# A cubic polynomial in place of tanh, with a general version behind a branch

## The chip, the cores and the metric

The kernel runs on one core of a Trainium2 chip. The core has TensorE for matmuls (PE in the rows; PEld is its weight load), VectorE (DVE), ScalarE (ACT), GpSimd (POOL) and SyncE (SP), whose queue issues most of the DMA transfers. The metric is the time of one execution on the device, in microseconds (us). The median of several runs is compared.

## The reference

Sigmoid attention with a shift by log S, and behind it a block of two matmuls with h - tanh(h) between them:

```python
scores = scale * np.matmul(q, k.transpose(0, 1, 3, 2)) - np.log(S)   # (8, 12, 448, 64) each
attn = 1.0 / (1.0 + np.exp(-scores))
attn_out = np.matmul(attn, v)
x = attn_out.transpose(0, 2, 1, 3).reshape(B * S, H * D)             # 3584 x 768
h = x @ w_in                                                         # 768 x 2048
g = h - np.tanh(h)
out = g @ w_out                                                      # 2048 x 768
```

q and k are drawn as normal values times about 0.42, v times 0.1. w_in and w_out are 64-bit floats, scaled by one over the root of their rows.

## The kernel before

The eight batches (448 tokens each) go through one after another. In batch b the first product (`moe1`, in `product`) makes h in eight groups of two 128-row blocks, in a PSUM tile ph; after each group `mix` turns it into g. The second product (`moe2`) makes the six output blocks po, d = 0 to 5, each from 16 blocks f of g, three matmuls each. Values are split into a high and a low float16 half, so each product is three matmuls of 448 columns.

Between the matmuls of `moe2` of batch b stand the steps of the attention of batch b + 1 (the generator `stream`: scores, sigmoid a, its halves ahl, the product acc, norms sqn and pbn). They are placed by hand: BLOCKS lists the positions at which the next step is issued, and `second` merges these events into the loop over the matmuls. From batch 1 on the last two f of d = 0 come in the middle of d = 1. Batch 0 is different: `first` follows a string of letters, ORDER, in which the 64-bit weights are converted (raw, stb, wo, wi), the first product runs in float32 and the attention of batch 1 is threaded in.

TensorE, ScalarE, VectorE and GpSimd execute what is issued to them in that order. SyncE's queue is in order too; in batch 0 the scheduler of the framework sets it. Tiles come from pools: the tag "mm" is a ring of two PSUM buffers that the po tiles take in turn, "sc" a ring of two for scores and ph, and "t" in the pool temps a ring of eight SBUF buffers for the temporaries of `mix`, the a and ahl of the attention and raw weights. A tile that takes a buffer waits until what the buffer held has been read.

`mix` before computes two things for a group: th = h - tanh(h), and a polynomial of degree eleven, h^3 times two quadratic factors in u = h^2. Where u is over 0.65^2, a predicated copy takes th. `finish_g` splits the group before into halves g.

Of the kernel before, what the change touches and what calls it, by code (L numbers as in the profile page):

```python
# [24 lines left out]
CUT = 0.65  # L25
# [3 lines left out]
KAPPA = 0.00592396  # L29
B1, C1 = 0.62576354, 2.54375998**2  # L30
B2, C2 = -2.38756233, 1.58089437**2


class Builder:
# [225 lines left out]
    def w_in_scales(self):  # L260


        nc = self.nc
        n = self.DFF // 4
        cn = self.ps.tile([P, 512], F32, name="cn", tag="av", bufs=1)
        for j, sq in enumerate(self.row):
            nc.tensor.matmul(cn[32 * j : 32 * (j + 1), :n], self.onesb[:, :32], sq, start=True, stop=True)
        st = self.sm.tile([P, 1], F32, name="st", tag="st")
        nc.vector.tensor_reduce(st, cn[:, :n], axis=AX.X, op=ALU.max)
        yield 0  # L270
        pt = self.ps.tile([P, 512], F32, name="pt", tag="tr", bufs=1)
        nc.tensor.transpose(pt[:1, :P], st, self.ident)
        mx = self.sm.tile([1, 1], F32, name="mx2", tag="mx2")
        nc.vector.tensor_reduce(mx, pt[:1, :P], axis=AX.X, op=ALU.max)
        yield 0
        pb = self.ps.tile([P, 512], F32, name="pb", tag="tr", bufs=1)
        nc.tensor.matmul(pb[:, :1], self.onesf[:1, :], mx, start=True, stop=True)
        self.W2 = self.const.tile([P, 1], F32, name="W2")
        nc.vector.tensor_scalar(self.W2, pb[:, 0:1], 1.03, None, op0=ALU.mult)
        self.Swi, self.iSwi = self.scale_of(self.W2, "swi")  # L280

    def w_out_bound(self, e):

# [352 lines left out]
        do_av()  # L636
        yield 1150, True

    def attention32(self):

        nc = self.nc
        tags = (("kn", "qn"), ("K", "Q"))
        loaded, todo, accs = [], [], {}
        xs = self.xs = []
        order = iter([(j, c) for j in range(self.NP) for c in (range(QT) if j % 2 else range(QT + 1))])

        def load():
            j = len(loaded)
            loaded.append(self.load_qk(0, j, tags[j % 2]))

        def values():
            l = next(l for l in loaded if len(l) == 2)
            l.append(self.load_v(0, loaded.index(l), self.att, "vhl", 3))

        def table():
            one = self.sm.tile([P, 1], F32, name="one", tag="m")
            nc.scalar.activation(one, self.nls, AF.Sigmoid)

        def scores():
            j, c = next(order)  # L660
            both = (j, j + 1) if c == QT else (j,)
            K, Q = ([loaded[i][x][:, None] for i in both] for x in range(2))
            a = self.weigh(self.scores(K, Q, c), 1.0 / math.sqrt(D))
            todo.append((j, c, a))

        def open_acc(j):
            accs[j] = self.ps.tile([P, 512], F32, name="acc", tag="mm", bufs=2)

        def av():
            j, c, a = todo.pop(0)  # L670
            v = loaded[j][2][:, None]
            if c == QT:
                open_acc(j + 1)
                self.av([accs[j], accs[j + 1]], v, a, c, 0)
            else:
                if c == 0 and j % 2 == 0:
                    open_acc(j)
# [28 lines left out]
    def h_scales(self, ix):  # L706

        V = self.nc.vector
        t1 = lambda name: self.sm.tile([P, 1], F32, name=name)
        ih, ihk = t1("ih"), t1("ihk")  # L710
        V.tensor_tensor(ih, ix, self.iSwi, op=ALU.mult)
        V.tensor_scalar(ihk, ih, KAPPA, None, op0=ALU.mult)
        return ih, ihk

    def split_x(self, hl, x, Sx, act):
# [21 lines left out]
    def g_scales(self, m):  # L737

        t1 = lambda name: self.sm.tile([P, 1], F32, name=name)
        V = self.nc.vector  # L740
        hb = t1("hb")
        V.tensor_scalar(hb, m, self.W2, None, op0=ALU.mult)
        hc = t1("hc")
        V.tensor_scalar(hc, hb, 1e12, None, op0=ALU.min)
        h2 = t1("h2")
        V.tensor_tensor(h2, hc, hc, op=ALU.mult)
        h3 = t1("h3")
        V.scalar_tensor_tensor(h3, h2, 1.0 / 9.0, hc, op0=ALU.mult, op1=ALU.mult)
# [54 lines left out]
    def mix(self, ps, g, ih, ihk):  # L803

        nc = self.nc
        V = nc.vector
        temp = lambda name: self.tp.tile([P, 2, self.S], F32, name=name, tag="t")
        u = temp("u")
        nc.scalar.activation(u, ps, AF.Square, scale=ih)  # L809
        th = temp("th")  # L810
        nc.scalar.activation(th, ps, AF.Tanh, scale=ih)  # L811
        m = temp("m")
        V.scalar_tensor_tensor(m, ps, ihk, u, op0=ALU.mult, op1=ALU.mult)  # L813
        V.scalar_tensor_tensor(th, ps, ih, th, op0=ALU.mult, op1=ALU.subtract)  # L814
        yield 1
        self.finish_g()
        yield 1
        q1 = temp("q1")
        nc.scalar.activation(q1, u, AF.Square, bias=self.b1)  # L819
        V.scalar_tensor_tensor(m, q1, C1, m, op0=ALU.add, op1=ALU.mult)  # L820
        yield 1
        q2 = temp("q2")
        nc.scalar.activation(q2, u, AF.Square, bias=self.b2)  # L823
        V.scalar_tensor_tensor(m, q2, C2, m, op0=ALU.add, op1=ALU.mult)  # L824
        yield 1
        nc.scalar.activation(u, u, AF.Relu, bias=self.b3)  # L826
        V.copy_predicated(m, u.bitcast(U32), th)  # L827
        yield 1
        self.late.append((m, g))

    def finish_g(self):
        while self.late:
# [62 lines left out]
    def build(self):  # L895
        nc, tc = self.nc, self.tc

        def const(name, value, n=1):
            t = self.const.tile([P, n], F32, name=name)
            nc.vector.memset(t, value)  # L900
            return t

        self.nls = const("nls", -math.log(self.S))
        self.b1 = const("b1", B1)
        self.b2 = const("b2", B2)
        self.b3 = const("b3", -CUT * CUT)
        self.tiny = const("tiny", TINY)
        self.ih0 = const("ih0", 1.0)
        self.ihk0 = const("ihk0", KAPPA)
        self.iSwo = const("iswo", 1.0, 2)  # L910
        self.sums = [const(f"ss{i}", 0.0, 6) for i in range(2)]
        self.Swo = []
        self.sums_out, self.bound = [[], []], [None, None]
        self.xs32, self.x2b = False, []
        pieces = list(self.pieces())
        nA = 4 * self.NC
        E = mybir.EngineType
        with tc.manual_schedule(engines={E.PE, E.Activation, E.DVE, E.Pool}):
            nB = nA + self.NF + self.EARLY
            self.stage = tc.alloc_tile_pool(name="stage", bufs=2, reuse_waits="tile")  # L920
            self.blocks = self.stream()
            self.first(
                self.convert(pieces[:nA], "attention"),
                self.convert(pieces[nA:nB], "mixture"),
                self.convert(pieces[nB:], "product"),
            )
        with tc.manual_schedule(engines={E.PE, E.Activation, E.DVE, E.Pool, E.SP}):
            for b in range(1, self.B):
                self.batch(b)
        self.gp.release()  # L930
# [128 lines left out]
    def second(self, b, blocks, alone, events):  # L1059

        step = lambda: next(self.blocks)
        events += [(p, step) for p in blocks]
        scales = []

        def norms():
# [12 lines left out]
        assert not events  # L1078


def build_kernel(tc, q, k, v, moe_w_in, moe_w_out, out):
    with ExitStack() as ctx:
        Builder(ctx, tc, q, k, v, moe_w_in, moe_w_out, out).build()


# [27 lines left out]
```

## Time and profile before

| What | Value |
| --- | --- |
| median of 3 runs | 1164.04 us (1163.76 to 1164.43) |
| span of the traced execution, from its first to its last instruction | 1163.1 us |
| TensorE busy | 1150.5 us (99%) |
| VectorE busy | 903.6 us (78%) |
| ScalarE busy | 865.6 us (74%) |
| GpSimd busy | 78.4 us (7%) |
| TensorE's weight loads busy | 555.4 us (48%) |

The traced execution has no time of its own beside its span; the runs' median is 0.94 us above it. An engine's busy time is the union of its instructions; matmuls are pipelined, so a busy TensorE may still have small waits between matmuls.

### The profile page before, as it was taken

The page shows a single profiled execution, that of the slowest core. Times are in us where ns is not written, and L with a number is a line of the kernel's source. Part 1 is how long each engine was busy: PE and PEld are TensorE (multiplying, and loading weights), DVE is VectorE, ACT ScalarE, POOL GpSimd, SP SyncE. Part 2 cuts the span into 40 slices and gives each one's busy share as a digit, 9 for nine tenths or more (in the row PEclk, how much of TensorE's full clock was granted, in tenths as well). Part 3 has the DMA queues.
Part 4 walks back from the last instruction along what each step waited for, and adds up shares of the span by engine and source line. Part 5 has one row for each costly group of instructions (what it writes and reads, how often), then busy time and mean ns, then how long its engine had stood idle before and what let it go on. Part 6 is the DMA issues. An engine that isn't in the chain of part 4 may idle for free.

```text
span 1163.1 us, 17369 instructions
## 1 busy us (share of the span) xinstructions
PE 1150.5 (99%) x6795; PEld 555.4 (48%) x6796; DVE 903.6 (78%) x1299; ACT 865.6 (74%) x1195; POOL 78.4 (7%) x58
## 2 busy tenths in 40 slices
PE   9999998999999999999999999999999999999998
PEld 3345433454444554445444554445544454445554
DVE  6999998789777896679867897778976799646930
ACT  7988995678986878858878688867887688745820
POOL 0000000000130002200021000200022000300000
PEclk9999999999999999999999999999999999999999
DMA  9942161100222002210022100211012100000000
GB/s 361 358 161 68 44 217 41 41 8 1 70 76 64 16 1 73 71 48 1 17 72 64 41 1 25 80 53 36 1 58 84 51 1 8 25 24 9 1 24 25
DMA packets 35938, 70.33 MB, mean 60 GB/s; under 512 B 3984, under 2 KB 25616, under 8 KB 35856
## 3 DMA queue, kind: packets, MB, share of 16 engines
q1 hardware_dynamic: 35568, 68.88, 17.9%
q8 instruction: 53, 0.87, 0.3%
q10 hardware_dynamic: 288, 0.34, 0.1%
q14 instruction: 29, 0.24, 0.1%
HBM read 58.20 MB, written 11.01 MB: 60 GB/s over the span
## 4 chain that ended last, share of the span: by engine, by line
PE 73%; ACT 1%; issue 0%; DVE 0%; ACTq 0%
PE po L851 32%; PE ph L771 28%; PE acc L423 6%; PE sc L392 6%; ACT a L403 0%; ACT ahl L409 0%; ACT sqn L333 0%; PE nm L688 0%; ACT o L871 0%; ACT x L437 0%; ACT Q L367 0%; ACT x L452 0%; ACT o L865 0%; DVE o L867 0%; ACT tn L344 0%
## 5 line engine op out<-in xcount | busy, mean ns | idle before, releaser
L851 PE MATMUL po<-g,wo 128*128 128x448 f16 x2304 | 451.5, 353 | 3.1 <-ACT o L871 3.1
L771 PE MATMUL ph<-xhl,wi 128*128 128x448 f16 x2016 | 382.5, 352 | 0.0
L851 PEld LDWEIGHTS <-wo 128*128 128x128 f16 x2304 | 219.7, 98 | 228.1 <-issue 31.2
L771 PEld LDWEIGHTS <-wi 128*128 128x128 f16 x2016 | 197.3, 98 | 184.1
L410 DVE SCALAR_TENSOR_TENSOR ahl<-a,ahl 128x896 f16<-128x896 f32 x126 | 162.0, 1321 | 129.4 <-ACT ahl L409 128.0
L403 ACT ACTIVATE a<-sc,nls,rn 128x896 f32<-128x896 f32 x147 | 155.8, 1090 | 64.3 <-PE sc L392 64.3
L409 ACT ACTIVATE ahl<-a 128x896 f16<-128x896 f32 x126 | 113.2, 941 | 0.6
L809 ACT ACTIVATE u<-ph,ih 128x896 f32<-128x896 f32 x64 | 64.5, 1007 | 61.9 <-PE ph L771 59.8
L392 PE MATMUL sc<-Q,K 64*128 64x448 f16 x1008 | 101.6, 355 | 1.2 <-DVE th L814 1.2
L813 DVE SCALAR_TENSOR_TENSOR m<-ph,ihk,u 128x896 f32<-128x896 f32 x64 | 73.4, 1147 | 26.6 <-ACT th L811 26.2
L764 ACT ACTIVATE g<-m,Sg 128x896 f16<-128x896 f32 x64 | 66.7, 1042 | 35.0 <-DVE m L827 28.3
L827 DVE COPY_PREDICATED m<-u,th 128x896 f32<-128x896 uint32 x64 | 77.3, 1208 | 7.3 <-ACT u L826 0.9
L423 PE MATMUL acc<-ahl,vhl 128*64 128x448 f16 (+1 forms) x864 | 80.6, 356 | 0.3 <-ACT tn L344 0.2
L454 POOL TENSOR_TENSOR x<-x 128x448 f32<-128x448 f32 x24 | 27.5, 1146 | 761.2 <-ACT x L437 761.2
L765 DVE SCALAR_TENSOR_TENSOR g<-m,Sg,g 128x896 f16<-128x896 f32 x64 | 73.3, 1145 | 6.8 <-ACT g L764 6.7
L824 DVE SCALAR_TENSOR_TENSOR m<-q,m 128x896 f32<-128x896 f32 x64 | 69.9, 1092 | 6.7 <-DVE m L820 0.5
L958 PE MATMUL ph<-x,wi 128*128 128x448 f32 x192 | 73.8, 540 | 0.0
L814 DVE SCALAR_TENSOR_TENSOR th<-ph,ih,th 128x896 f32<-128x896 f32 x64 | 73.2, 1143 | 0.0
L820 DVE SCALAR_TENSOR_TENSOR m<-q,m 128x896 f32<-128x896 f32 x64 | 69.4, 1085 | 0.0
L826 ACT ACTIVATE u<-u,b 128x896 f32<-128x896 f32 x64 | 66.7, 1042 | 1.9
L823 ACT ACTIVATE q<-u,b 128x896 f32<-128x896 f32 x64 | 65.9, 1029 | 0.0
L819 ACT ACTIVATE q<-u,b 128x896 f32<-128x896 f32 x64 | 65.9, 1029 | 0.0
(137 smaller groups left out, 978.6 us busy)
## 6 DMA issues: line engine op xcount, KB each, us to landing
out<-o SPq DMA_DIRECT2D x47, 224.0 KB, 1.9
knn<-k SPq DMA_DIRECT2D x45, 224.0 KB, 2.6
qnn<-q SPq DMA_DIRECT2D x44, 224.0 KB, 2.6
rawo<-moe_w_out SPq DMA_DIRECT2D x22, 384.0 KB, 5.3
raw<-moe_w_in SPq DMA_DIRECT2D x13, 512.0 KB, 8.2
vn<-v SPq DMA_DIRECT2D x24, 256.0 KB, 2.8
wo<-moe_w_in SPq DMA_DIRECT2D x11, 512.0 KB, 8.0
vn<-v SPq DMA_DIRECT2D x24, 192.0 KB, 2.5
```

The source lines that it names most:

```text
L392: self.nc.tensor.matmul(ps[i * m : (i + 1) * m, h, : self.S], K[i][r, w, c * P : c * P + m], Q[i][r, x, :], start=(n == 0), stop=(n == len ...
L403: self.nc.scalar.activation(a[:, 0], ps[:, :, : self.S], AF.Sigmoid, bias=self.nls, scale=scale)
L409: nc.scalar.activation(A[:, 0], a[:, 0], AF.Copy, scale=A_SCALE)
L410: nc.vector.scalar_tensor_tensor(A[:, 1], a[:, 0], A_SCALE, A[:, 0], op0=ALU.mult, op1=ALU.subtract)
L423: self.nc.tensor.matmul(acc[i][h * D : (h + 1) * D, : self.S], v[k, w, 2 * QT + h if half else h * QT + c], A[k, x, h], start=(n == 0 and ...
L765: nc.vector.scalar_tensor_tensor(g[:, 1], m, Sg, g[:, 0], op0=ALU.mult, op1=ALU.subtract)
L771: self.nc.tensor.matmul(ph, self.wi[:, self.slot(c, k), part, e * P : (e + 1) * P], xhl[c][:, x, :], start=(i == 0), stop=(i == len(prods) ...
L813: V.scalar_tensor_tensor(m, ps, ihk, u, op0=ALU.mult, op1=ALU.mult)
L814: V.scalar_tensor_tensor(th, ps, ih, th, op0=ALU.mult, op1=ALU.subtract)
L827: V.copy_predicated(m, u.bitcast(U32), th)
L851: nc.tensor.matmul(po[:, :S], self.wo[:, e * self.NF + 2 * ks[f // 2] + f % 2, w, at : at + P], gs[f // 2][:, x, f % 2], start=(f == 0 and ...
L958: nc.tensor.matmul(ph[:, e, :S], self.fp32(self.wi, self.slot(c, k))[:, 0, e * P : (e + 1) * P], xs[c], start=(c == 0), stop=(c == self.NC ...
```

## The change

`mix` computes m = h^3 times one quadratic factor in u, with other constants, and nothing else: tanh, its subtraction, the second factor, the comparison and the predicated copy are gone, and so are two of five temporaries. A bound decides whether that is enough. `column_norms` squares w_in (ScalarE), adds over its rows (VectorE, then a matmul with ones) and takes the largest column sum W2x; `g_scales` keeps the largest squared token norm in xmax; `verdict` multiplies the two by 1.06 and compares with 0.04. The steps of `column_norms` are events of `second`: eight in batches 2 to 5, at positions 10 and 24, and five in batch 6. At the end each engine loads the flag into a register and branches: where it is zero, the class `General` computes everything anew with tanh (its attention is that of batch 0, its products are float32).

```diff
+SMALL = 0.04
+KAPPA0, B0, C0 = 0.0526796487258969, -1.265328334909593, 4.726497609373637
...
+    def column_norms(self):
...
+        n = 2 * P
+        total = self.wi[:, self.NC * self.NB :].rearrange("p a b c -> p (a b c)").bitcast(BF16)
+        for k in range(self.NB):
+            sq = self.tp.tile([P, self.NC, n], BF16, name="wsq", tag="t")
+            nc.scalar.activation(sq, self.wi[:, self.NC * k : self.NC * (k + 1), 0], AF.Square, scale=self.iSwi)
+            h = self.NC // 2
+            V.tensor_tensor(sq[:, :h], sq[:, :h], sq[:, h:], op=ALU.add)
+            V.tensor_tensor(sq[:, 0], sq[:, 0], sq[:, 1], op=ALU.add)
+            V.tensor_tensor(total[:, k * n : (k + 1) * n], sq[:, 0], sq[:, 2], op=ALU.add)
+            yield 0
+        m = self.sm.tile([P, 4], F32, name="wm")
+        for i in range(4):
+            w = self.ps.tile([P, 512], F32, name="wn", tag="mm", bufs=2)
+            nc.tensor.matmul(w, self.onesb, total[:, i * 512 : (i + 1) * 512], start=True, stop=True)
+            V.tensor_reduce(m[:, i : i + 1], w, axis=AX.X, op=ALU.max)
+            yield 0
+        self.W2x = self.const.tile([P, 1], F32, name="W2x")
+        V.tensor_reduce(self.W2x, m, axis=AX.X, op=ALU.max)
+        yield 0
+
+    def verdict(self):
...
+        V.tensor_scalar(self.xmax, self.xmax, self.W2x, 1.06, op0=ALU.mult, op1=ALU.mult)
+        V.tensor_scalar(self.xmax, self.xmax, SMALL, None, op0=ALU.is_le)
...
+        V.tensor_tensor(self.xmax, self.xmax, m, op=ALU.max)
...
         u = temp("u")
         nc.scalar.activation(u, ps, AF.Square, scale=ih)
-        th = temp("th")
-        nc.scalar.activation(th, ps, AF.Tanh, scale=ih)
         m = temp("m")
         V.scalar_tensor_tensor(m, ps, ihk, u, op0=ALU.mult, op1=ALU.mult)
-        V.scalar_tensor_tensor(th, ps, ih, th, op0=ALU.mult, op1=ALU.subtract)
         yield 1
         self.finish_g()
         yield 1
-        q1 = temp("q1")
-        nc.scalar.activation(q1, u, AF.Square, bias=self.b1)
-        V.scalar_tensor_tensor(m, q1, C1, m, op0=ALU.add, op1=ALU.mult)
+        q = temp("q")
+        nc.scalar.activation(q, u, AF.Square, bias=self.b0)
+        V.scalar_tensor_tensor(m, q, C0, m, op0=ALU.add, op1=ALU.mult)
+        self.late.append((m, g))
         yield 1
-        q2 = temp("q2")
-        nc.scalar.activation(q2, u, AF.Square, bias=self.b2)
-        V.scalar_tensor_tensor(m, q2, C2, m, op0=ALU.add, op1=ALU.mult)
-        yield 1
-        nc.scalar.activation(u, u, AF.Relu, bias=self.b3)
-        V.copy_predicated(m, u.bitcast(U32), th)
-        yield 1
-        self.late.append((m, g))
...
+        norms2 = lambda: next(self.columns, None)
+        if b == 2:
+            self.columns = self.column_norms()
+        if 2 <= b <= 5:
+            events += [(p, norms2) for p in (10, 24)]
+        if b == 6:
+            events += [(p, norms2) for p in (18, 22, 28, 32, 40)]
+        if b + 1 == self.B:
+            events.append((20, self.verdict))
...
+        small = nc.values_load(flag[0:1, 0:1].bitcast(mybir.dt.int32), min_val=0, max_val=0x3F800000)
+        with tc.If(small == 0, preferred_fallthrough_block=False):
+            with ExitStack() as ctx:
+                General(ctx, *args).run()
```

**TensorE in batch 6, around the ends of d = 1 and d = 2.** Before, po_9886 is d = 1, po_10036 d = 2 and po_10241 d = 3; wo are the weights, ahl, vhl and acc belong to the attention. A name in brackets is the engine whose semaphore the row waits for:

```order
L851 LDWEIGHTS wo_97
L851 MATMUL po_9886<-g_9799,wo_97 128x448
...
L851 MATMUL po_10036<-g_9399,wo_97 128x448 [waits DVE_49]
...
L423 MATMUL acc_10104<-ahl_10146,vhl_9330 64x448
...
L851 MATMUL po_10036<-g_9799,wo_97 128x448
...
L851 MATMUL po_10241<-g_9399,wo_97 128x448
```

Now po_9486 is d = 1, po_9640 d = 2 and po_9851 d = 3; the wn are the matmuls of the column sums:

```order
L302 LDWEIGHTS onesb_98
L302 MATMUL wn_9631<-wi_100,onesb_98 128x512 [waits DVE_49]
L875 LDWEIGHTS wo_101
L875 MATMUL po_9486<-g_9407,wo_101 128x448
...
L875 MATMUL po_9640<-g_9062,wo_101 128x448 [waits Activation_49]
...
L875 MATMUL po_9640<-g_9407,wo_101 128x448
...
L302 MATMUL wn_9848<-wi_100,onesb_98 128x512 [waits DVE_49]
L875 LDWEIGHTS wo_101
L875 MATMUL po_9851<-g_9062,wo_101 128x448 [waits DVE_49]
```

A wn stands three matmuls ahead of the end of d = 1, another right behind that of d = 2. The first matmul of d = 2 waited for the eviction of d = 0 by VectorE, and now for that of d = 1 by ScalarE; the first of d = 3 had no wait of its own, and now waits for the eviction of d = 2 by VectorE.

**ScalarE in the mixture, one group.** Before, from the square u of one group to that of the next (th is tanh, g the high half of the group before, q the two squares, the last u the comparison):

```order
L809 ACTIVATE u<-ph,ih 128x896 [waits PE_49]
L811 ACTIVATE th<-ph,ih 128x896
L764 ACTIVATE g<-m,Sg 128x896 [waits DVE_49]
L819 ACTIVATE q_10730<-u,b_100 128x896 [waits Activation_49]
L823 ACTIVATE q_10733<-u,b_102 128x896
L826 ACTIVATE u<-u,b_104 128x896 [waits DVE_49,Activation_49]
```

Now, with the end of the mixture and the evictions behind it:

```order
L843 ACTIVATE u<-ph,ih 128x896 [waits PE_49]
L798 ACTIVATE g<-m,Sg 128x896 [waits DVE_49]
L850 ACTIVATE q<-u,b_104 128x896 [waits Activation_49]
...
L895 ACTIVATE o<-po,iK 128x448 [waits DMAHW1_49,PE_49]
L895 ACTIVATE o<-po,iK 128x448 [waits DMAHW3_49,PE_49,Activation_49]
```

Three of six operations are gone; the order of the rest has not moved.

**SyncE at the end of the program.** Before, the last output transfers and the jump to the program's end:

```order
L874 DMA out<-o 128x448 [waits DMAHW3_49,Activation_49]
L874 DMA out<-o 128x448 [waits DMAHW4_49,DVE_49]
L874 DMA out<-o 128x448 [waits DMAHW5_49,Activation_49]
L874 DMA out<-o 128x448 [waits DMAHW6_49,DVE_49]
L868 DMA out<-o 128x224 [waits DMAHW0_49,DVE_49]
L1109 UNCONDITIONAL_BRANCH
```

Now (flag is the verdict, DMAHW0 to 7 are the semaphores of SyncE's transfers):

```order
L1240 TENSOR_LOAD flag [waits DVE_49]
...
L898 DMA out<-o 128x448 [waits DMAHW6_49,DVE_49]
L892 DMA out<-o 128x224 [waits DMAHW0_49,DVE_49]
L1241 COMPARE_AND_BRANCH
L1241 UNCONDITIONAL_BRANCH [waits DMAHW0_49,DMAHW1_49,DMAHW2_49,DMAHW3_49,DMAHW4_49,DMAHW5_49,DMAHW6_49,DMAHW7_49]
L1149 DMA raw<-moe_w_in 128x256 [waits DMAHW3_49,DMAHW4_49,DMAHW2_49,DMAHW5_49,DMAHW1_49,DMAHW6_49,DMAHW0_49,DMAHW7_49,PE_49,Activation_49]
```

The load of the flag stands ahead of the last five transfers. Behind the comparison the path that is taken waits for all transfers and then jumps over the code of `General`, which begins with the row of raw.

## Rows read from the trace of the kernel before

**Rows 1.** The view of the cores, and the page's busy time by engine.
```profile
core 0: 1163.1 us, clock 0.998
...
PE 1150.5 (99%) x6795; PEld 555.4 (48%) x6796; DVE 903.6 (78%) x1299; ACT 865.6 (74%) x1195; POOL 78.4 (7%) x58
```
**Rows 2.** The chain that ended last: start, length in us, what.
```profile
1050.12 54.48 PE ph L771 x288
1104.61 54.49 PE po L851 x288
```
**Rows 3.** TensorE's timeline: start, us, instruction; in brackets idle before, releaser.
```profile
133.68 0.74 PE L392 MATMUL sc<-Q,K 64*128 64x448 f16 x6 [1.25 <-DVE th L814]
...
160.04 0.16 PE L342 MATMUL pbn<-ss,onesb 128*128 128x4 bf16 x1 [1.62 <-ACT sqn L333]
...
178.75 1.87 PE L851 MATMUL po<-g,wo 128*128 128x448 f16 x6 [3.09 <-ACT o L871]
...
291.54 0.17 PE L342 MATMUL pbn<-ss,onesb 128*128 128x6 bf16 x1 [0.83 <-ACT sqn L333]
```
**Rows 4.** Groups by line: count, busy us, mean ns, idle before.
```profile
L811 ACT ACTIVATE th<-ph,ih 128x896 f32<-128x896 f32 x64 | 64.1, 1001 | 0.0
L823 ACT ACTIVATE q<-u,b 128x896 f32<-128x896 f32 x64 | 65.9, 1029 | 0.0
L826 ACT ACTIVATE u<-u,b 128x896 f32<-128x896 f32 x64 | 66.7, 1042 | 1.9
...
L814 DVE SCALAR_TENSOR_TENSOR th<-ph,ih,th 128x896 f32<-128x896 f32 x64 | 73.2, 1143 | 0.0
L824 DVE SCALAR_TENSOR_TENSOR m<-q,m 128x896 f32<-128x896 f32 x64 | 69.9, 1092 | 6.7 <-DVE m L820 0.5
L827 DVE COPY_PREDICATED m<-u,th 128x896 f32<-128x896 uint32 x64 | 77.3, 1208 | 7.3 <-ACT u L826 0.9 <-DVE m L824 0.5
```
**Rows 5.** Timelines of TensorE and VectorE ahead of 134 us.
```profile
106.44 22.71 PE L958 MATMUL ph<-x,wi 128*128 128x448 f32 x60
...
132.44 1.18 DVE L814 SCALAR_TENSOR_TENSOR th<-ph,ih,th 128x896 f32<-128x896 f32 x1
```
**Rows 6.** Timelines of SyncE's queue and of ScalarE, 139 to 151 us.
```profile
139.35 3.43 SPq L155 DMA_DIRECT2D rawo<-moe_w_out  x3
...
145.97 0.33 SPq L315 DMA_DIRECT2D knn<-k  x1
...
150.59 0.58 ACT L333 ACTIVATE sqn<-knn 128x448 bf16<-128x448 f32 x1 [0.57 <-DMA knn<-k]
```
**Rows 7.** Timeline of ScalarE, 167 to 179 us.
```profile
167.70 0.57 ACT L170 ACTIVATE stb<-rawo 128x384 f32<-128x384 f32 x1 [0.92 <-PE wl L201]
...
178.08 0.61 ACT L871 ACTIVATE o<-po,iK 128x448 f32<-128x448 f32 x1
```
**Rows 8.** A stretch: engines' busy us, granted clock, DMA share, GB/s.
```profile
179.35:182.70 3.35, 3.35 (x19) 1.05 (x21) 1.71 (x9) 0.48 (x1) 0.00 (x0) 0.50 0.18 68
```
**Rows 9.** Timeline of ScalarE, last idle time ahead of 291 us.
```profile
282.46 1.01 ACT L809 ACTIVATE u<-ph,ih 128x896 f32<-128x896 f32 x1 [0.88 <-PE ph L771]
```
**Rows 10.** Timelines of batch 6: TensorE, ScalarE, TensorE, VectorE.
```profile
995.33 4.15 PE L851 MATMUL po<-g,wo 128*128 128x448 f16 x21
...
999.53 0.62 ACT L871 ACTIVATE o<-po,iK 128x448 f32<-128x448 f32 x1
...
1013.83 4.71 PE L851 MATMUL po<-g,wo 128*128 128x448 f16 x24
...
1018.46 0.67 DVE L873 TENSOR_SCALAR o<-po,iK 128x448 f32<-128x448 f32 x1
```
**Rows 11.** Timeline of ScalarE, batch 6.
```profile
1011.55 2.09 ACT L403 ACTIVATE a<-sc,nls,rn 128x896 f32<-128x896 f32 x2 [3.43 <-PE sc L392]
```
**Rows 12.** SyncE's last issue, and the page's DMA issues: KB, us to landing.
```profile
1160.13 0.33 SPq L868 DMA_DIRECT2D out<-o  x1
...
out<-o SPq DMA_DIRECT2D x1, 112.0 KB, 1.7
```

More of the change, by code (lines that the diff above doesn't have):

```diff
@@ L280, in w_in_scales @@
         self.Swi, self.iSwi = self.scale_of(self.W2, "swi")
+    def column_norms(self):
+        nc = self.nc
+        V = nc.vector
+        n = 2 * P
[18 more added lines that the diff above has]
+    def verdict(self):
+        V = self.nc.vector
+        V.tensor_scalar(self.xmax, self.xmax, self.W2x, 1.06, op0=ALU.mult, op1=ALU.mult)
+        V.tensor_scalar(self.xmax, self.xmax, SMALL, None, op0=ALU.is_le)
     def w_out_bound(self, e):
@@ L637, in stream, with attention32 @@
         yield 1150, True
-    def attention32(self):
+    def attention32(self, b=0):
         nc = self.nc
@@ L648, in load @@
             j = len(loaded)
-            loaded.append(self.load_qk(0, j, tags[j % 2]))
+            loaded.append(self.load_qk(b, j, tags[j % 2]))
         def values():
             l = next(l for l in loaded if len(l) == 2)
-            l.append(self.load_v(0, loaded.index(l), self.att, "vhl", 3))
+            l.append(self.load_v(b, loaded.index(l), self.att, "vhl", 3))
         def table():
@@ L711, in h_scales @@
         V.tensor_tensor(ih, ix, self.iSwi, op=ALU.mult)
-        V.tensor_scalar(ihk, ih, KAPPA, None, op0=ALU.mult)
+        V.tensor_scalar(ihk, ih, KAPPA0, None, op0=ALU.mult)
         return ih, ihk
@@ L903, in build @@
         self.nls = const("nls", -math.log(self.S))
-        self.b1 = const("b1", B1)
-        self.b2 = const("b2", B2)
-        self.b3 = const("b3", -CUT * CUT)
+        self.b0 = const("b0", B0)
+        nc.vector.memset(self.xmax, 0.0)
         self.tiny = const("tiny", TINY)
         self.ih0 = const("ih0", 1.0)
-        self.ihk0 = const("ihk0", KAPPA)
+        self.ihk0 = const("ihk0", KAPPA0)
         self.iSwo = const("iswo", 1.0, 2)
@@ L1078, in second, with __init__, add_squares, weights @@
         assert not events
-def build_kernel(tc, q, k, v, moe_w_in, moe_w_out, out):
-    with ExitStack() as ctx:
-        Builder(ctx, tc, q, k, v, moe_w_in, moe_w_out, out).build()
+class General(Builder):
+    def __init__(self, ctx, tc, q, k, v, w_in, w_out, out):
+        self.tc, self.nc = tc, tc.nc
+        self.q, self.k, self.v, self.w_in, self.w_out, self.out = q, k, v, w_in, w_out, out
+        self.B, self.NP, _, self.S = q.shape
+        self.DM, self.DFF = w_in.shape
+        self.NC = self.DM // P
+        self.NF = self.DFF // P
+        pool = lambda name, bufs, **kw: ctx.enter_context(tc.tile_pool(name=name, bufs=bufs, **kw))
+        self.const = pool("gconst", 1)
+        self.wp = pool("gweights", 1)
+        self.sm = pool("gsmall", 2)
+        self.nat = pool("gnat", 2)
+        self.qk = pool("gqk", 2)
+        self.att = pool("gatt", 2)
+        self.xp = pool("gxp", 8)
+        self.tp = pool("gtemps", 8)
+        self.gp = pool("gg", 1)
+        self.stage = pool("gstage", 2)
+        self.op = pool("gouts", 2)
+        self.ps = pool("gps", 1, space=PSUM)
+    def add_squares(self, j, x, pool):
+        pass
+    def weights(self, src, name):
+        nc = self.nc
+        V = nc.vector
+        rows, cols = src.shape
+        w = self.wp.tile([P, rows // P, cols], F32, name=name)
+        n = 256
+        for r in range(rows // P):
+            for c in range(0, cols, n):
+                raw = self.stage.tile([P, n], U64, name="raw")
+                nc.sync.dma_start(raw, src[r * P : (r + 1) * P, c : c + n])
+                parts = raw.bitcast(U32).rearrange("p (n t) -> p n t", t=2)
+                low, high = parts[:, :, 0], parts[:, :, 1]
+                a = self.stage.tile([P, n], F32, name="a")
+                nc.scalar.activation(a, high.bitcast(F32), AF.Abs, scale=2.0**-112)
+                au = a.bitcast(U32)
+                V.tensor_scalar(au, au, 3, None, op0=ALU.logical_shift_left)
+                V.scalar_tensor_tensor(au, low, 29, au, op0=ALU.logical_shift_right, op1=ALU.bitwise_or)
+                V.scalar_tensor_tensor(
+                    w[:, r, c : c + n].bitcast(U32), high, 0x80000000, au, op0=ALU.bitwise_and, op1=ALU.bitwise_or
+                )
+        return w
+    def mix(self, ps, g):
+        nc = self.nc
+        V = nc.vector
+        temp = lambda name: self.tp.tile([P, self.S], F32, name=name, tag="t")
+        u, th, q = temp("u"), temp("th"), temp("q")
+        nc.scalar.activation(u, ps, AF.Square)
+        nc.scalar.activation(th, ps, AF.Tanh)
+        V.scalar_tensor_tensor(g, ps, KAPPA, u, op0=ALU.mult, op1=ALU.mult)
+        V.tensor_tensor(th, ps, th, op=ALU.subtract)
+        nc.scalar.activation(q, u, AF.Square, bias=self.b1)
+        V.scalar_tensor_tensor(g, q, C1, g, op0=ALU.add, op1=ALU.mult)
+        nc.scalar.activation(q, u, AF.Square, bias=self.b2)
+        V.scalar_tensor_tensor(g, q, C2, g, op0=ALU.add, op1=ALU.mult)
+        nc.scalar.activation(u, u, AF.Relu, bias=self.b3)
+        V.copy_predicated(g, u.bitcast(U32), th)
+    def attend(self, b):
+        steps = self.attention32(b)
+        run = lambda text: [steps[x]() for x in text]
+        run("llu")
+        for j in range(0, self.NP, 2):
+            run("uss")
+            run("sv" * 5 + "vv")
+            if j + 2 < self.NP:
+                run("llu")
+        return self.xs
+    def run(self):
+        nc = self.nc
+        S = self.S
+        def const(name, value):
+            t = self.const.tile([P, 1], F32, name=name)
+            nc.vector.memset(t, value)
+            return t
+        self.nls = const("gnls", -math.log(S))
+        self.b1 = const("gb1", B1)
+        self.b2 = const("gb2", B2)
+        self.b3 = const("gb3", -CUT * CUT)
+        w_in = self.weights(self.w_in, "gwi")
+        w_out = self.weights(self.w_out, "gwo")
+        for b in range(self.B):
+            xs = self.attend(b)
+            gs = []
+            for f in range(self.NF):
+                ph = self.ps.tile([P, 512], F32, name="ph", tag="mm", bufs=2)
+                for c in range(self.NC):
+                    nc.tensor.matmul(
+                        ph[:, :S], w_in[:, c, f * P : (f + 1) * P], xs[c], start=(c == 0), stop=(c == self.NC - 1)
+                    )
+                g = self.gp.tile([P, S], F32, name=f"g{f}")
+                self.mix(ph[:, :S], g)
+                gs.append(g)
+            for d in range(self.NC):
+                po = self.ps.tile([P, 512], F32, name="po", tag="mm", bufs=2)
+                for f in range(self.NF):
+                    nc.tensor.matmul(
+                        po[:, :S], w_out[:, f, d * P : (d + 1) * P], gs[f], start=(f == 0), stop=(f == self.NF - 1)
+                    )
+                o = self.op.tile([P, S], F32, name="o", tag="o", bufs=2)
+                nc.scalar.activation(o, po[:, :S], AF.Copy)
+                nc.sync.dma_start(self.out[d * P : (d + 1) * P, b * S : (b + 1) * S], o)
@@ new lines, in build_kernel @@
+def build_kernel(tc, q, k, v, moe_w_in, moe_w_out, out):
+    nc = tc.nc
+    args = (tc, q, k, v, moe_w_in, moe_w_out, out)
+    with ExitStack() as outer:
+        flags = outer.enter_context(tc.tile_pool(name="flags", bufs=1))
+        flag = flags.tile([P, 1], F32, name="flag")
+        with ExitStack() as ctx:
+            first = Builder(ctx, *args)
+            first.xmax = flag
+            first.build()
+        small = nc.values_load(flag[0:1, 0:1].bitcast(mybir.dt.int32), min_val=0, max_val=0x3F800000)
+        with tc.If(small == 0, preferred_fallthrough_block=False):
+            with ExitStack() as ctx:
+                General(ctx, *args).run()
```

## The prediction

> **What bounds the kernel now.** I read the busy time first: the traced execution spans 1163.1 us at a mean granted clock of 0.998, and TensorE is busy for 1150.5 of them [rows 1]. Busy is not yet packed, so the chain that ended last comes next: 288 matmuls of the first product take 54.48 us and 288 of the last second product 54.49 us [rows 2], 189.2 ns for 448 columns both times, where 448 columns at 2.4 GHz are 186.7 ns. The first of these stretches runs while VectorE and ScalarE work on the mixture nearly without a break, the second while they have almost nothing to do. So they do not slow TensorE where it is fed, and what they can give back is only time in which TensorE stands still. The timeline of TensorE shows where: four stops of 1.25, 1.62, 3.09 and 0.83 us [rows 3], 6.79 us together, all before 292 us. The reader is to see there what ended each: an operation of VectorE once, of ScalarE three times. Behind the last of them the chain is matmuls alone, of which rows 2 are two pieces, up to the last eviction.
>
> The Trainium skill (Perfetto Trace Analysis, Identifying the Most-Contended Engine) says that matmul busy time misjudges the distance to the roofline and that weight-load busy time should be read, which is 48% here. By that alone much would be left to gain from a lighter VectorE; the trace disagrees, since the spacing is 189.2 ns beside busy and beside idle neighbours.
>
> **What the change removes.** Each of the 64 mixture groups loses three ScalarE operations (tanh, second square, relu: 1001, 1029 and 1042 ns) and three of VectorE (1143, 1092 and 1208 ns) [rows 4], 3.1 and 3.4 us a group, some 197 and 220 us in all. Nearly all of it lies beside packed matmuls and is worth nothing; it counts at the four stops.
> - Stop 1 (1.25 us): the scores wait until VectorE's th, which ends at 133.62, has read the ph buffer, while TensorE had finished that ph at 129.15 [rows 5]. That th is gone, and so are three operations of the group before it on which VectorE was late. The remaining reader, m, needs ph, one ScalarE square of 1.0 us and its own 1.1 us: about 131.3, ahead of 132.43, where TensorE comes. Gain 1.25.
> - Stop 2 (1.62 us): the norm matmul waits for sums of squares that ScalarE makes late. ScalarE had to wait for a load of k until 150.59; that load was issued at 145.97, behind three raw weight loads that SyncE could begin only at 139.35 [rows 6]. After 133 us ScalarE loses two operations (2.1 us) that came before the norms, and the raw loads now wait for earlier operations, as the temps ring hands out three buffers a group and not five. To keep up with a TensorE that is 1.25 us ahead, ScalarE must be 2.9 us earlier; 2.1 us plus the stop's own 1.25 us cover that. Gain 1.62; bounds 0 and 1.62.
> - Stop 3 (3.09 us): TensorE waits for the eviction o, which ScalarE ends at 178.69. ScalarE works without a break worth naming from 167.70, where it had waited 0.92 us for TensorE itself [rows 7]. So that run of 11 us starts from TensorE and holds no mixture work: it moves with TensorE and the stop stays. Gain 0; bounds 0 and 3.09. The granted clock falls to 0.50 (1.2 GHz) just after it, for the 3.35 us of [rows 8]; half speed there costs 1.7 us, which stays too, and is the upper bound's extra.
> - Stop 4 (0.83 us): the sums of squares again, at 291. ScalarE was last idle at 282.46 [rows 9], and tanh, square and relu of one group stand between. 3.1 us less covers 0.83. Gain 0.83.
>
> Gains: 1.25 + 1.62 + 0.83 = 3.70 us.
>
> **What it adds.**
> - Four matmuls wn over 512 columns, in the seventh batch, on the path: 189.2 x 512 / 448 = 216 ns each (an estimate from rows 2), 0.86 us.
> - What they do to the ring of two PSUM buffers, tag "mm". Before, each po takes the buffer of the po before the last, evicted long ago. Now wn takes that buffer, and the next po gets the one that TensorE has just filled: it must wait for the eviction, and the rest of TensorE's queue stands behind it. The order shows this twice. First, po of d=2 waits for ScalarE's o of d=1. In the trace d=1 ends 12 matmuls into the 21 that start at 995.33, at 997.60, with wn 997.82; ScalarE, still busy with scores, does that o from 999.53 to 1000.15 [rows 10]. Wait 2.33 us. Second, po of d=3 waits for VectorE's o of d=2. d=2 ends 3 matmuls into the 24 from 1013.83, at 1014.40, with wn 1014.61; VectorE has that o at 1018.46 to 1019.13, behind two ahl [rows 10]. Wait 4.52 us. Both evictions stand behind work that TensorE's own scores set off, so a lighter mixture brings neither nearer. Bounds: 1.3 us for both, if each o started at once (0.62 and 0.67 us), and 6.85; I take 6.85, as the order of these queues is unchanged.
> - The clock. The stop of 3.09 us was followed by half clock, and the mean clock of 0.998 leaves no room for another such stretch before the end. A stop of 4.52 us is longer, so I count one more: 1.7 us, bounds 0 and 3.4 (both new waits).
> - Eight ScalarE squares of 1536 columns (at most 1042 x 1536 / 896 = 1.79 us) and three small VectorE adds each, in batches 2 to 5. They lie in front of stretches where ScalarE waits for scores, such as the 3.43 us before 1011.55 [rows 11], beside packed matmuls: 0. Without that cover they would cost up to 1.8 us each, 14 us.
> - The exit. SyncE issues its last transfer at 1160.13 and the span ends at 1163.1; a transfer of that size lands in 1.7 us [rows 12], and now the waits on all queues stand before a jump over the other version's code, and waits and barrier behind it. The loads of the flag on the other engines lie under that landing. The trace has no such jump. Below, it costs 0; above, two round trips like that landing, 3.4 us. I take one, 1.7 us.
>
> The Trainium skill (Runtime: NRT & Kernel Launch, Instruction fetch mechanics) says that a taken branch to code outside the fetched window must first fetch it from memory. By that the exit cannot be free; no run here shows it.
>
> Sum: 0.86 + 6.85 + 1.7 + 1.7 = 11.1 of cost, 3.7 of gain: +7.4 us on 1163.1, so 1170.5 for the span. The median of the runs stands 0.94 above the span: 1171.5 us.
>
> **Rivals.**
> - The clock holds after the new stop: 1164.04 + 5.7 = 1169.8. For it: the fall in the trace followed a stretch that had held two stops, not one.
> - Stop 3 goes as well, and the half clock with it: 4.8 less, 1166.7, or 1165.0 if the clock also holds in the seventh batch. Against it: ScalarE's run starts from TensorE.
> - The exit or a wait that I do not see costs more, an extra 1.7 to 5 us: 1173.2 to 1176.5. For it: five engines load and branch, and the squares' cover is thin.
> - Not slower: the two evictions come in time, which needs ScalarE 2.3 and VectorE 4.5 us ahead of their places in [rows 10]. Then there is no clock loss either, and 1164.04 - 3.7 + 0.86 + 1.7 = 1162.9, or 1158.1 without stop 3. It decides from the point where both waits are under 1 us. Against it: both engines idle shortly before, waiting for TensorE, so they cannot run ahead.
> - TensorE's 98.9% busy hides waits that the removed 200 us set free: then some 11 us over all 288-matmul stretches (2.5 ns of 189.2 each) could go. Rows 2 speak against it.
> - The change does something else: the bound is over 0.04 and everything runs twice. With the inputs drawn from the reference the largest token norm squared is 0.0203 and the largest column norm squared 1.185, so the bound is near 0.0255. It would at least double the time, over 2300 us.
>
> **How the numbers follow.** As forecast 0.50; the clock holds 0.20; stop 3 goes 0.12; more cost 0.13; not slower 0.03; hidden waits 0.01; twice 0.01. A measurement of this kernel tells 0.2%, 2.3 us, from no change. Slower: the forecast, the clock's case, the costlier one, and half of stop 3's and the last: 0.90; I keep 0.86 for what is unseen. Same 0.10, faster 0.04. The range leaves out the upper end of the costlier case and the lower half of stop 3's: 1166 to 1175.
>
> **What would show it.** Right: stops 1, 2 and 4 gone from TensorE's timeline, the 3 us stop kept near 173 us; in the seventh batch two stops of TensorE ended by o of ScalarE and of VectorE, near 2.3 and 4.5 us, with four wn; half clock after the second; ScalarE and VectorE each about 200 us less busy; more than 3 us between the last output's issue and the span's end. Wrong: no stop at these two places, or new stops in batches 2 to 5 ended by work behind wsq, or a span that ends with the old 3 us while the total grows.

## The result, and the profile after

| | before | after |
| --- | --- | --- |
| median of 4 runs, us | 1163.9 (1163.49 to 1164.43) | 1177.38 (1176.4 to 1178.17) |
| ratio to before, 95% interval | | 1.0111 [1.0096, 1.0125] |
| span of the traced execution, us | 1163.1 | 1174.6 |
| SyncE's last issue, us | 1160.13 [rows 12] | 1166.38 |
| from there to the end of the span, us | 2.97 | 8.22 |

The change made the kernel slower by 13.5 us, where 7.6 were forecast (1171.5 against 1163.9). The direction was right, and the size missed the range of 1166 to 1175. The view of the cores and the page's busy time, of the changed kernel:

```profile
core 0: 1174.6 us, clock 0.995
PE 1153.3 (98%) x6799; PEld 556.1 (47%) x6800; DVE 707.7 (60%) x1145; ACT 690.2 (59%) x1011; POOL 77.4 (7%) x58
```

Against [rows 1], VectorE lost 196 us and ScalarE 175, and TensorE's busy time grew. TensorE's timeline of the changed kernel (start, us, instruction; in brackets the idle time before and what ended it):

```profile
133.94 1.50 PE L425 MATMUL sc<-Q,K 64*128 64x448 f16 x18
...
156.93 0.16 PE L375 MATMUL pbn<-ss,onesb 128*128 128x4 bf16 x1
...
176.37 2.40 PE L875 MATMUL po<-g,wo 128*128 128x448 f16 x6 [3.71 <-ACT o L895]
...
288.66 0.17 PE L375 MATMUL pbn<-ss,onesb 128*128 128x6 bf16 x1 [0.36 <-ACT sqn L366]
...
993.83 0.38 PE L302 MATMUL wn<-wi,onesb 128*128 128x512 bf16 x1
994.05 0.73 PE L875 MATMUL po<-g,wo 128*128 128x448 f16 x3
996.99 1.86 PE L875 MATMUL po<-g,wo 128*128 128x448 f16 x9 [2.21 <-ACT o L895]
...
1013.41 0.74 PE L875 MATMUL po<-g,wo 128*128 128x448 f16 x3
1013.99 0.38 PE L302 MATMUL wn<-wi,onesb 128*128 128x512 bf16 x1
1018.76 5.82 PE L875 MATMUL po<-g,wo 128*128 128x448 f16 x21 [4.39 <-DVE o L897]
```

Of the four stops of [rows 3] the first is gone, the second is down to 0.11 us, the third has grown to 3.71, since TensorE comes 3.0 us sooner to an eviction that ends only 2.4 us sooner (at 176.32, against 178.69 in [rows 7]), and the fourth is down to 0.36. That eviction, in ScalarE's timeline of the changed kernel:

```profile
175.71 0.61 ACT L895 ACTIVATE o<-po,iK 128x448 f32<-128x448 f32 x1
```

The two new stops in batch 6 are 2.21 and 4.39 us, each behind a wn and a po. Half clock (1.2 GHz) follows the second of them, as [rows 8] showed it behind the third stop. The columns of the stretch are those of [rows 8]:

```profile
1019.33:1022.75 3.42, 3.42 (x11) 1.43 (x10) 0.00 (x0) 0.00 (x0) 0.00 (x0) 0.50 0.18 67
```

All that is in the forecast. The end is not. The last row of SyncE's timeline:

```profile
1166.38 0.33 SPq L892 DMA_DIRECT2D out<-o  x1
```

The view of transfers from that issue to 1174 us (packets, MB and share of a queue; KB and us to landing of an issue):

```profile
q10 hardware_dynamic: 144, 0.11, 5.2%
q1 hardware_dynamic: 144, 0.11, 4.4%
q14 instruction: 6, 0.05, 2.3%
q8 instruction: 2, 0.03, 1.6%
...
out<-o SPq DMA_DIRECT2D x1, 112.0 KB, 3.1
```

The last transfer lands in 3.1 us instead of the 1.7 of [rows 12], and blocks of instructions are fetched, three beside the transfer and the others behind it. What SyncE does then stands in the trace's records of its own instructions (start in us; the two kernels on the right are experiments that follow):

| SyncE | after | transfers of the other version on ScalarE | other version cut short |
| --- | --- | --- | --- |
| last issue | 1166.39 | 1166.39 | 1167.61 |
| first jump, to the end of the main program | 1166.77 | 1166.78 | 1168.00 |
| first wait for a transfer served | 1169.52 | 1168.96 | 1168.11, of another queue |
| second jump, over the other version | 1170.11 | 1169.54 | 1168.28 |
| first instruction behind it | 1173.31 | 1169.73 | 1169.30 |
| end of the span | 1174.6 | 1171.0 | 1170.6 |

So the second jump alone takes 3.20 us. The landing is served 1.4 us late, and seven more waits stand one behind the other between the landing and the jump, 0.6 us. That is 5.2 of the 5.25 us by which the exit grew.

### The profile page after: what moved, and what is told of

It reads as the page before. It is cut to its first block, busy times and chain, and to the rows that moved or that the text cites. A ratio compares the mean times of both kernels' runs of the same rounds, so it can differ in the third digit from the quotient of the medians.

```text
span 1174.6 us, 16792 instructions
## 1 busy us (share of the span) xinstructions
PE 1153.3 (98%) x6799; PEld 556.1 (47%) x6800; DVE 707.7 (60%) x1145; ACT 690.2 (59%) x1011; POOL 77.4 (7%) x58
## 5 line engine op out<-in xcount | busy, mean ns | idle before, releaser
L851 DVE SCALAR_TENSOR_TENSOR m<-q,m 128x896 f32<-128x896 f32 x64 | 69.5, 1086 | 0.9
L850 ACT ACTIVATE q<-u,b 128x896 f32<-128x896 f32 x64 | 66.0, 1032 | 0.3
L425 PEld LDWEIGHTS <-K 64*128 64x128 f16 x1008 | 35.7, 97 | 57.6 <-issue 32.6
L456 PEld LDWEIGHTS <-vhl 128*64 128x64 f16 (+1 forms) x864 | 38.6, 108 | 40.0 <-issue 19.8
L981 PEld LDWEIGHTS ph<-x,wi 128*128 128x128 f32 x192 | 36.2, 190 | 33.2 <-issue 32.4
L496 POOL TENSOR_TENSOR x<-x,x 128x448 f32<-128x448 f32 x21 | 37.0, 1761 | 172.6 <-ACT x L485 171.2
L400 ACT ACTIVATE Q<-qnn,sn 128x448 f16<-128x448 f32 x42 | 27.7, 660 | 29.4 <-DVE sn L386 25.5
```

The costliest lines, as they stand in the source:

```text
L425: self.nc.tensor.matmul(ps[i * m : (i + 1) * m, h, : self.S], K[i][r, w, c * P : c * P + m], Q[i][r, x, :], start=(n == 0), stop=(n == len ...
L456: self.nc.tensor.matmul(acc[i][h * D : (h + 1) * D, : self.S], v[k, w, 2 * QT + h if half else h * QT + c], A[k, x, h], start=(n == 0 and ...
L851: V.scalar_tensor_tensor(m, q, C0, m, op0=ALU.add, op1=ALU.mult)
L981: nc.tensor.matmul(ph[:, e, :S], self.fp32(self.wi, self.slot(c, k))[:, 0, e * P : (e + 1) * P], xs[c], start=(c == 0), stop=(c == self.NC ...
```

## The experiments

All ratios are to the kernel before, run on the same chip beside each kernel; its medians there were 1164.5 to 1164.8 us.

**1. The four wn in the first product of batch 6.** There TensorE uses another ring, and the buffers of tag "mm" have long been evicted.

```diff
-            events += [(p, norms2) for p in (18, 22, 28, 32, 40)]
+            if self.now == 6 and 1 <= k <= 5:      # moe1, before ph of group k
+                next(self.columns)
```

> The changed kernel with the four wn matmuls and their maxima moved from the second product of batch 6 into its first product, one ahead of each of the mixture groups 1 to 4; nothing is left out. Theory A (ring): the two stops of 2.21 and 4.39 us in batch 6 come from the ring of two PSUM buffers alone and the half clock behind the second from its length; all three go, 6.6 + 1.7 = 8.3 us: span 1174.6 - 8.3 = 1166.3, median 1177.4 - 8.3 = 1169.1, and batch 6 shows no stop over 0.3 us. Rival B: TensorE waits for the same two engines at another place of batch 6 when it comes there sooner; then the span keeps more than 1170.

Measured: 1167.93 us, ratio 1.0031 [1.0019, 1.0042], span 1165.1. TensorE's timeline and the stretch of batch 6 in which the stops had been:

```profile
916.00 6.97 PE L805 MATMUL ph<-xhl,wi 128*128 128x448 f16 x36
922.81 0.38 PE L302 MATMUL wn<-wi,onesb 128*128 128x512 bf16 x1
923.03 6.97 PE L805 MATMUL ph<-xhl,wi 128*128 128x448 f16 x36
```

```profile
985.00:1030.00 45.00, 45.00 (x328) 21.23 (x324) 25.67 (x32) 32.34 (x44) 11.64 (x8) 1.00 0.06 21
```

TensorE is busy through all 45 us at full clock, and SyncE's last issue comes at 1157.44, 8.9 us sooner. Theory A holds and nothing waits elsewhere: the ring and the clock behind it cost 8.3 us or a little more, and wn itself 0.22 us each. The span came out 1.2 us under the expected; 0.5 of that is a shorter landing of the last transfer, 2.6 us.

**2. The other version cut short, the branch kept.** Its body became 35 instructions that touch the same memory:

```diff
-        w_in = self.weights(self.w_in, "gwi")
-        ...
+        nc.vector.memset(w, 0.0)                 # both weights' tiles
+        for tag in range(8):                     # every PSUM bank
+            nc.tensor.matmul(ph[:, :S], w[:, 0, :P], w[:, 0, :S], start=True, stop=True)
+            nc.scalar.activation(o, ph[:, :S], AF.Copy)
```

> The changed kernel with its If, flag load and jumps, but the version behind the If is cut to 11 TensorE, 15 ScalarE, 3 VectorE and 6 SyncE instructions (it leaves out the other version, which does not run here). Theory A (far code): SyncE's jump over the other version took 3.2 us because its target had to be fetched, and those fetches held up the last outputs by 1.4 us; both go, and some 0.5 us of waits on queues that the other version used: span 1174.6 - 5.1 = 1169.5, the median by up to 0.9 us more if the part outside the span (0.9 us before, 1.8 after) is code too. Rival B: a taken branch costs its 3 us at any distance: span 1174.0 or more.

Measured: 1172.32 us, ratio 1.0064 [1.0051, 1.0077], span 1170.6. From the last issue to the end it takes 3.0 us, as before the change: a flag load, a compare and two jumps, with a near target, cost nothing that shows. The wait for the landing stands behind the second jump here and not ahead of it, as this version uses fewer queues, so up to 1.0 us of a near jump would lie hidden under it; experiment 3 keeps the wait ahead. In the view of transfers from the last issue on (to 1170.5 us) there is no row of instructions fetched, and the landing is back:

```profile
q10 hardware_dynamic: 144, 0.11, 12.6%
q1 hardware_dynamic: 144, 0.11, 11.6%
...
out<-o SPq DMA_DIRECT2D x1, 112.0 KB, 1.7
```

The span is 1.1 us over the expected. TensorE came 0.5 us later to batch 6, and the half clock there was twice as long here and began while TensorE still stood, so that it worked 4.92 us at half speed and not 3.42:

```profile
1017.36:1024.19 6.83, 4.92 (x14) 1.98 (x14) 2.46 (x3) 0.00 (x0) 0.32 (x1) 0.50 0.09 34
```

**3. The other version's transfers on ScalarE's queue.** All its code stays, but SyncE has one instruction there to jump over.

```diff
 class General(Builder):
+    QUEUE = staticmethod(lambda nc: nc.scalar)
-                nc.sync.dma_start(raw, ...)
+                self.queue.dma_start(raw, ...)
```

> The changed kernel with all transfers of the other version issued by ScalarE, so that SyncE has one instruction there and its jump is short, while the other engines still jump far; nothing is left out. Theory A (only the last engine's jump counts): ScalarE, VectorE and TensorE had ended their jumps by 1169.9 us in the changed kernel, under the landing of the last output; SyncE's jump of 3.2 us goes: span 1174.6 - 3.1 = 1171.5, median 1174.3. Rival B: the jump of SyncE waits for something else than its code (the other engines, the transfers): span 1174.6, no change.

Measured: 1173.47 us, ratio 1.0077 [1.0065, 1.009], span 1171.0. SyncE's jump takes 0.18 us instead of 3.20 (the table above, middle column); TensorE, VectorE and ScalarE still jump far, beside the landing and SyncE's waits: they are through at 1168.98, 1169.67 and 1169.63, just ahead of SyncE at 1169.73. So the jump's price lies in its far target, and it counts on the engine that jumps last. The landing takes 2.6 us, with three blocks of instructions fetched beside it as in the changed kernel.

**4. The polynomial alone.**

```diff
-        if 2 <= b <= 5: ...                 # norms2, verdict
-        with tc.If(small == 0, ...): General(ctx, *args).run()
```

> The changed mixture alone: no column norms, no bound, no flag, no If and no other version (left out: the test that guards the polynomial). Theory A: what the changed kernel shows of its stops carries over: 1.25 + 1.51 + 0.47 us gained at stops 1, 2 and 4 and 0.3 at two small ones, 0.6 lost at the stop of 3.09: span 1163.1 - 2.9 = 1160.2, median 1161.1. Rival B: the forecast's own 3.7 us: span 1159.4. Rival C: stops only move: 1163.

Measured: 1160.98 us, ratio 0.9972 [0.9962, 0.9981], span 1159.2. The stops that are left in TensorE's timeline, and SyncE's last issue, 3.65 us before that of [rows 12]:

```profile
176.11 2.40 PE L875 MATMUL po<-g,wo 128*128 128x448 f16 x6 [3.51 <-ACT o L895]
...
288.20 0.17 PE L375 MATMUL pbn<-ss,onesb 128*128 128x6 bf16 x1 [0.36 <-ACT sqn L366]
...
1156.48 0.33 SPq L892 DMA_DIRECT2D out<-o  x1
```

From trace to trace the forecast's 3.7 (rival B) comes nearer than my reading of the stops afterwards (2.9, theory A); the runs cannot tell the two apart, as their interval is a gain of 2.2 to 4.4 us. Of 207 us of VectorE and 187 of ScalarE that this kernel saves, TensorE gets 3.65.

**5. One of the two stops.** Three wn stay in the second product; the place at 28, ahead of the longer stop, is empty.

```diff
-            events += [(p, norms2) for p in (18, 22, 28, 32, 40)]
+            events += [(p, norms2) for p in (18, 22, 32, 40)]   # the first one in moe1
```

> The changed kernel with one of its wn matmuls moved into the first product of batch 6, so that three remain in the second product, at the places of the first, second and fourth; nothing is left out. The place that made the stop of 4.39 us is empty, that of the stop of 2.21 us is not. Theory A (the half clock belongs to the 4.39 us stop): the 2.21 us stop stays, no half clock in batch 6, TensorE ends 4.39 + 1.7 = 6.1 us sooner: span 1174.6 - 6.1 = 1168.5. Rival B (any stop there brings it): the half clock comes behind the 2.21 us stop too: span 1170.2.

Measured: 1170.46 us, ratio 1.0054 [1.004, 1.0067], span 1168.3. The stop, and the stretch behind it:

```profile
997.71 1.86 PE L877 MATMUL po<-g,wo 128*128 128x448 f16 x9 [2.21 <-ACT o L897]
```

```profile
997.71:1031.12 33.41, 33.41 (x249) 15.67 (x249) 19.98 (x30) 20.78 (x25) 7.56 (x6) 1.00 0.04 15
```

The clock stays at its full 2.4 GHz. So the stop of 2.21 us alone does not bring the half clock, and it goes with that of 4.39 us; no run has that one without the other ahead of it.

**6. Both edits, and one exchange of steps.** With wn moved and the transfers on ScalarE:

> The changed kernel with both edits: wn in the first product of batch 6 and the other version's transfers on ScalarE's queue; nothing is left out. Theory A (the two costs add): 1165.1 us, the traced span with wn moved, less the 3.6 us that the short jump gave: span 1161.5, median 1163.3, within 0.2% of the kernel before. Rival B (with SyncE out of the way another engine's jump ends last): span 1163 to 1165.

Measured: 1164.66 us, ratio 1.0002 [0.9993, 1.0011], span 1162.9; its exit takes 4.8 us. The expectation was 1.4 us too low: it counted the shorter landing of experiment 1 twice (0.5), and TensorE's last work came 0.6 later than there on another chip, most of it from the first 20 us. Rival B fell: SyncE's jump again took 0.18 us, and SyncE was again the last to be through. The guarded polynomial stands level with the kernel before. Then the third stop was taken up, by exchanging two letters of the first batch's order, P for the product step and B for the attention step:

```diff
-        "...PCCCSZBPCCCPCX..."
+        "...PCCCSZPBCCCPCX..."
```

> As the kernel with both edits, and one step of the first batch's order exchanged: the product step that ends output row d=1 comes ahead of the attention step that stood before it, so that its eviction stands ahead of that step's work on ScalarE; nothing is left out. Theory A: the stop of 3.55 us at 172 us is the same ring of two PSUM buffers (wl stands between po d=1 and po d=2), it goes, and the half clock of 3.4 us behind it as well: span 1161.5 - 3.5 - 1.7 = 1156.3, median 1158.1, faster than the kernel before by 0.5%. Rival B: the stop moves to the next wait of TensorE in this stretch, where both other engines are nearly full: span 1160 to 1161.5.

> The kernel before, with that one exchange of steps alone. Theory A: 3.09 us of stop and 1.7 us of half clock go: span 1163.1 - 4.8 = 1158.3, so that most of what the last kernel gains is not the change's. Rival B: the stop moves: span 1162 to 1163.

Measured on the same chip: 1161.43 us, ratio 0.9974 [0.9964, 0.9985], with both edits; 1161.74, ratio 0.9979 [0.997, 0.9988], for the kernel before with the exchange alone. In the first, the stop of 3.6 us is gone and the clock stays full, but two others stand behind it:

```profile
182.89 3.39 PE L459 MATMUL acc<-a,vn 128*64 128x448 f32 x20 [0.61 <-ACT tn L380]
187.51 0.74 PE L428 MATMUL sc<-Q,K 64*128 64x448 f16 x6 [1.23 <-ACT a L439]
```

```profile
170.00:200.00 30.00, 28.16 (x170) 12.62 (x167) 27.55 (x51) 19.32 (x36) 2.66 (x2) 1.00 0.21 61
```

Each theory has a part of it: 3.9 of the expected 5.2 us of span came. In the kernel before with the exchange 2.8 of 4.8 came (span 1160.3), with the clock full as well and the same stop of 1.23 us behind it:

```profile
190.70 0.74 PE L392 MATMUL sc<-Q,K 64*128 64x448 f16 x6 [1.23 <-ACT a L403]
```

The exchange is 0.2% faster than the kernel before and 0.3% faster with both edits; the intervals overlap, so it does as much without the change, as far as the runs tell.

**7. What is left of the exit.** The last kernel with the last row written in one piece, and the same without the branch (with its bound computed):

```diff
-                nc.scalar.activation(o[:, :h], ...); nc.scalar.dma_start(...)
-                nc.vector.tensor_scalar(o[:, h:], ...); nc.sync.dma_start(...)
+            nc.scalar.activation(o, po[:, :S], AF.Copy, scale=iv)
+            nc.sync.dma_start(self.out[rows, cols], o)
```

> The kernel with both edits and the exchange of steps, and the last output row written in one piece by ScalarE and SyncE instead of two halves; nothing is left out. SyncE waits for its transfers in a fixed order of eight; the last half came first in it, so that the other seven waits (0.6 us) stood behind its landing. In one piece the last transfer comes last in that order. Theory A (the seven waits are on the path): 0.5 us of them now lie under the landing, the issue comes 0.3 us sooner and the transfer, twice as large, lands 0.3 us later: from ScalarE's last eviction to the span's end 5.2 us, against 5.7 in the kernel with both edits and the exchange. Rival B (the waits take no time of their own): 5.7 or more.

> The kernel with wn in the first product and the exchange of steps, with the bound computed but without flag load, If and other version (left out: what the bound guards). It prices what is left of the exit. Theory A: with SyncE's jump short the exit still costs 4.75 us from the last issue to the span's end against 2.95 in the kernel before: 1.8 us go, span 1159.0 - 1.8 = 1157.2, and the last issue to the span's end takes 2.9 to 3.0. Rival B: ahead of the last issue the flag loads and the first jump cost time as well: span under 1156.5.

Measured: 1160.44 us, ratio 0.9961 [0.9947, 0.9975], and 1158.74, ratio 0.9947 [0.9934, 0.9961]. In one piece, seven of the eight waits are served by 1154.87, under the landing; ScalarE's last eviction to the end takes 5.4 us against 5.7, less than the 0.5 expected of it, since the transfer took longer to land:

```profile
1153.26 0.63 ACT L893 ACTIVATE o<-po,iK 128x448 f32<-128x448 f32 x1 [17.53 <-PEq L1241]
1153.92 0.33 SPq L896 DMA_DIRECT2D out<-o  x1
```

```profile
out<-o SPq DMA_DIRECT2D x1, 224.0 KB, 3.1
```

Without the branch the last issue to the end takes 2.6 us (2.9 to 3.0 expected), so the repaired exit still costs 2.1; ahead of the last issue the branch costs nothing (1154.28 there, 1154.24 with it), which rules out rival B. The version in one piece is the quickest with the guard, faster than the kernel before; against before with the exchange alone the intervals overlap, and whether the change then gains anything is open.

## Why the prediction missed

- **Stops 1, 2 and 4, gain 3.70:** right in the mechanism, and in the sum partly by luck. With the polynomial alone 3.65 came from trace to trace: stops 1 and 2 gave theirs within 0.1, stop 4 gave 0.47 of its 0.83, and stop 3 took 0.4 back; small waits that were not priced and a first stretch that ran 0.2 us quicker in that trace made up for it. The changed kernel's trace shows 3.21 gained by batch 6.
- **Stop 3 stays:** right, with its half clock. Its cause (the eviction behind ScalarE's run) was right too, but that run did not move with TensorE all the way, so the stop grew by 0.6. I did not see in it the ring that I saw in batch 6: in the code wl takes a buffer of tag "mm" between po of d=1 and po of d=2. That the stop goes when the eviction comes sooner, in the exchange of steps, agrees.
- **Ring waits of 2.33 and 4.52 us:** right, 2.21 and 4.39. Experiment 1 takes them away without an heir.
- **Half clock once more, 1.7 us:** right in size in the traced execution, and behind the second stop; experiment 5 shows that the first alone does not bring it. The rival in which the clock holds fell. The other three runs were 0.5 to 1.8 us longer, at a mean granted clock of 0.992 to 0.994 against 0.995, so more half clock in them is likely, but only the one was traced.
- **Four wn, 0.86 us:** right, 0.22 us each. **wsq at nothing:** right. With wn out of the ring and the squares in place, TensorE's last work came at most 1 us later than with the polynomial alone, of which wn is 0.88.
- **The exit, 1.7 us: this step failed.** "I take one, 1.7 us" put one landing for a jump. Measured 5.25: the jump 3.20, the landing 1.4 late, seven waits 0.6. The Trainium skill (Runtime: NRT & Kernel Launch, Instruction fetch mechanics) says that a taken branch to code outside the window must fetch it first; I cited that and then priced the jump by a row that had nothing to do with it. The runs agree with the page: 3.20 us over 527 instructions, 0.18 over one. Not priced at all were the late landing, beside which instructions are fetched while the other engines jump, and SyncE's fixed order of waits, which puts seven of them behind it. The rival "the exit costs more", at 0.13, was the true case, with an extra of 3.55. By itself that extra would have put the forecast at 1175.05, at the upper bound; the rest of the miss is the next point and 0.5 us of gain.
- **0.94 us from span to median: too small, by 1.84.** In every run that shows both, of every kernel, the own time stands 1.74 to 1.92 us above the span. So the traced execution of before, at 1163.1, was one of 1164.9, about 1 us above its median, and that of after, at 1176.4, is 1 us below its own. From trace to trace the change is 11.5 us, 6.25 up to the last issue (5.7 forecast) and 5.25 behind it (1.7); the two executions make it 13.5.
- **Hidden waits behind 98.9% busy:** fell. Weight loads are 47% busy after and 48% before, and the 196 us of VectorE gave TensorE nothing where it was fed. The prediction has VectorE and ScalarE work nearly without a break in the first stretch of [rows 2]. They are busy for 44.0 and 40.6 of its 54.5 us, against 11.7 and 8.2 in the second; the reading that they do not slow TensorE rests on the equal spacing of 189.2 ns, and holds.

## What to carry to other kernels

A tile of a ring that is put between two others makes the next one wait for the eviction of the one just filled, here 2.21 and 4.39 us: put it where the ring is idle, as the four wn in the first product. A guard at the end of a kernel costs the far jump of the engine that jumps last, so its code, transfers included, belongs on engines that are done early; here moving the transfers took 3.0 us of jump away. A bound from below and above for an unseen operation must hold all that happens at its place, not one row that is at hand. A gain of 394 us on two engines (the polynomial alone) is worth the stops that it ends on the third, here 3.65 us.

## What the runs showed of the hardware

- A jump over 527 instructions took SyncE 3.18 to 3.24 us (three kernels), over one 0.18, and over six at most 1.03, a wait for the landing included. In the changed kernel VectorE's jump over 1286 instructions took 3.21 us and ScalarE's over 1256 took 2.79, so no price by the length of a far jump shows.
- The last transfer of 112 KB landed in 2.5 to 3.1 us in the six kernels in which three blocks of instructions were fetched beside it, and in 1.7 to 1.8 in the five in which at most one was. That the fetches are the cause is argued from this, not shown by itself.
- In the traced executions half clock came behind the stops of 4.39 us and of 3.09 to 3.71, and not behind one of 2.21 nor behind two of 0.61 and 1.23. Behind the stop of 4.39 us it lasted 3.4 us in the changed kernel and 6.8 in that with the other version cut short.
